# Layer two's odd linear part computed once per token pair: 512 columns become 257, the mirrored half moves to VectorE and GpSimd

## The chip, the cores and the metric

The kernel runs on one core of a Trainium2 chip. A core has TensorE (matmuls, PE in the profile), VectorE (DVE), ScalarE (ACT), GpSimd (POOL) and SyncE (SP, which here only issues DMAs). The engines run side by side; each takes its instructions in the order in which the program gives them, and waits on semaphores where it needs another's result. [...] The metric is the device time of one execution in microseconds.

## The reference

```python
X = np.fft.fft(x, axis=1)          # x: 8 sequences, 3072 tokens, 256 features
X = np.fft.fft(X, axis=2)
a = X.real.reshape(24576, 256)
h = np.maximum(np.maximum(a @ w1, a @ w2), a @ w3)   # 256 -> 768
out = h @ w_out                                      # 768 -> 256
```

So it is a two-dimensional Fourier transform of each sequence, of which the real part goes through a feed-forward layer with a maximum of three projections. The kernel uses two identities. First, max(a w1, a w2, a w3) = a w1 + max(0, a (w2-w1), a (w3-w1)), so that the output is a linear part, a (w1 w_out), plus a hidden part through the 768 features. Second, token s and its mirror token 3072-s of a sequence share their parts: with an even part E and an odd part O, one is made of E + O and the other of E - O. Every matrix is folded with the feature transform beforehand, so the kernel never forms the full transform.

## The kernel before, in words

**Data.** For each of the 8 sequences the class Mix produces a tile t with the even parts tE and the odd parts tO of 1536 token pairs, 128 feature rows each. Row 0 of tO is an exception: it holds the transform's feature 128, which is even, so its sign does not turn for the mirrored token. The constant sgn (line 357) is +1 for row 0 and -1 for the others.

**Blocks, units, slots.** The main loop (line 707) goes over the sequences, and within one over 3 blocks of 512 token pairs. A block has 6 units, one for each group of 128 hidden features; I number them 0 to 5 (and 0 to 17 over a sequence, where the text says "units 13, 15, 17"). A unit is layer one for that group: unit_plus (lines 476, 477) makes the sums of the direct tokens in two PSUM banks with four matmuls; unit_out (490, 491) takes ReLU on ScalarE (tile stmp) and a maximum on VectorE, into hp. unit_minus (484) then adds a difference to the same two banks, of the unit before, which turns them into the sums of the mirrored tokens; unit_out makes hm of these. There are two pairs of banks for this, which the units use in turn.

**Layer two.** A block's layer two, l2_block, runs during the next block's units. It is a Python generator that hands TensorE one matmul for each step; each unit takes ten steps (l2_some(10), line 737), after its own layer one. It goes over the block's 4 slots of 128 token pairs, 0 to 3. For a pair of slots the even linear part is computed into a bank pl (516) and copied to SBUF by ScalarE (even, 520). Per slot a bank po takes: the odd linear part of the direct and of the mirrored tokens in a single matmul of 512 columns (524), the left 256 with the odd weights, the right 256 with the same weights times sgn; then six hidden matmuls of 256 columns from hp into the left half, and six from hm into the right half (500). VectorE adds the even part to both halves (ot, 529). po has two banks, used in turn by the slots (pool ps_o, 644). Two outputs leave: the right half by an indirect DMA that GpSimd issues (534), the left by a DMA on SyncE's queue (544). The last block has a routine of its own, l2_last, so that l2_block handles 23 blocks and 92 slots.

**What else stands in the queues.** After its layer-two steps a unit runs what the plan (line 666 on) puts there: the mix pieces of the next sequence (TensorE, with an eviction on ScalarE; 13 units of 18 have one, units 5 to 17 in most sequences), loads of later sequences on SyncE's queue, and turn_chunk, which casts a quarter of the next but one sequence's rows from fp32 to bf16 on GpSimd, in two instructions (144, 146). For sequences 2 and later these casts are planned in units 13, 15, 17 and unit 1 of the next sequence, or, while sequences 0 and 1 are worked on, in units 14, 16 and units 0 and 2 of the next; sequence 1's own casts are in units 0, 2, 5 and 8 of sequence 0. The order on every engine is the order of these calls: the kernel schedules by hand (line 57).

```python
                l2_some(10)                              # 737, in every unit
            nc.tensor.matmul(po, to[:, cp], gw[:, 256:768], start=True, stop=True)   # 524
```

Of the kernel before, what the change touches and what calls it, by code (L numbers as in the profile page):

```python
# [9 lines left out]
FP32 = mybir.dt.float32  # L10
# [3 lines left out]
ALU = mybir.AluOpType  # L14
# [19 lines left out]
def kernel(  # L34
# [46 lines left out]
    gE = [consts.tile([128, DFF], BF16, name=f"gE{i}", tag=f"gE{i}") for i in range(2)]  # L81
    gO = [consts.tile([128, DFF], BF16, name=f"gO{i}", tag=f"gO{i}") for i in range(2)]
    gD = [consts.tile([128, DFF], BF16, name=f"gD{i}", tag=f"gD{i}") for i in range(2)]
    gw = consts.tile([128, 768], BF16, tag="gw")
    rows_m = consts.tile([128, 12 * B], INT32, tag="rows_m")
    mark = consts.tile([1, 1], FP32, tag="mark")
    sgn = consts.tile([128, 1], FP32, tag="sgn")
    dif = consts.tile([128, 1], FP32, tag="dif")
    t_mid = consts.tile([128, 2, B], BF16, tag="t_mid")
    z_all = consts.tile([128, 128 * 26], BF16, tag="z_all")  # L90
    z = z_all.rearrange("p (c r) -> p c r", r=26)
# [119 lines left out]
    for (name, value) in (("half_pi", 0.5 * math.pi), ("rnd", ROUND), ("n24", -24.0)):  # L211
        c = gen.tile([128, 1], FP32, name=name, tag=name)
        nc.vector.memset(c, value)
        consts_of[name] = c
    nc.vector.memset(z[:, :, 24:26], 0.0)
    nc.vector.memset(m0f[:, 50:52], 0.0)
    nc.vector.memset(m0r[:, 50:52], 0.0)
    half = gen.tile([128, 256], FP32, tag="half")
# [169 lines left out]
    def prep_second():  # L388

        for jp in range(NJC // 2):  # L390
            pst = ps_f.tile([128, 512], FP32, name="pst", tag="ps")
            for k in range(2):
                jc = jp * 2 + k
                for fc in range(2):
                    nc.tensor.matmul(
                        pst[:, k * 256:(k + 1) * 256],
                        w1_bf[:, fc * DFF + jc * 128: fc * DFF + jc * 128 + 128],
                        md[fc], start=(fc == 0), stop=(fc == 1))
            nc.vector.tensor_copy(out=g1t[:, jp * 512:(jp + 1) * 512], in_=pst)
            yield  # L400
        psw = ps_f.tile([128, 512], FP32, name="psw", tag="ps")
        for half in range(2):
            for jc in range(NJC):
                nc.tensor.matmul(
                    psw[:, half * 256:(half + 1) * 256],
                    g1t[:, jc * 256 + half * 128: jc * 256 + half * 128 + 128],
                    wout_bf[:, jc * 256:(jc + 1) * 256],
                    start=(jc == 0), stop=(jc == NJC - 1))
        nc.vector.tensor_copy(out=gw[:, 0:512], in_=psw)
        nc.scalar.activation(out=gw[:, 512:768], in_=psw[:, 256:512], func=AX.Copy, scale=sgn)  # L410
        yield

    class Mix:
# [84 lines left out]
    def l2_hidden(po, hcols):  # L498
        for jc in range(NJC):
            nc.tensor.matmul(po, hcols(jc), wout_bf[:, jc * 256:(jc + 1) * 256],  # L500
                             start=False, stop=(jc == NJC - 1), skip_group_check=True)
            yield

    def l2_block(b, blk, hp, hm, te, to):

        base = b * S
        for sub in range(4):
            slot = blk * 4 + sub
            r = slot + 1
            cp = slice(slot * 128, slot * 128 + 128)  # L510
            sp = slice(sub * 128, sub * 128 + 128)
            if sub % 2 == 0:
                pl = ps_f.tile([128, 512], FP32, name="pl", tag="ps")
                for i in range(2):
                    ci = (slot + i) * 128
                    nc.tensor.matmul(pl[:, i * 256:(i + 1) * 256], te[:, ci:ci + 128],  # L516
                                     gw[:, 0:256], start=True, stop=True)
                    yield
                even = even_pool.tile([128, 512], FP32, name="even", tag="even")
                nc.scalar.copy(out=even, in_=pl)  # L520
            lin = even[:, (sub % 2) * 256:(sub % 2 + 1) * 256]
            po = ps_o.tile([128, 512], FP32, name="po", tag="po")
            ot = out_pool.tile([128, 512], FP32, name="ot", tag="ot")
            nc.tensor.matmul(po, to[:, cp], gw[:, 256:768], start=True, stop=True)  # L524
            yield
            yield
            yield from l2_hidden(po[:, 0:256], lambda jc: hp[:, jc, sp])
            yield from l2_hidden(po[:, 256:512], lambda jc: hm[:, jc, sp])
            nc.vector.tensor_tensor(  # L529
                out=ot.rearrange("p (h c) -> p h c", h=2),  # L530
                in0=po.rearrange("p (h c) -> p h c", h=2),
                in1=lin.unsqueeze(1).to_broadcast([128, 2, 256]), op=ALU.add)
            lo = 1 if r == 12 else 0
            stored(nc.gpsimd.indirect_dma_start(  # L534
                out, bass.IndirectOffsetOnAxis(
                    ap=rows_m[0:128 - lo, b * 12 + slot: b * 12 + slot + 1], axis=0),
                ot[lo:128, 256:512], None), "scattered", ("scattered", "direct"))
            nc.gpsimd.memset(mark, 0.0)
            if r <= 11:
                stores = [(0, 128, base + r)]  # L540
            else:
                stores = [(0, 64, base), (64, 128, base + 12)]
            for (p0, p1, row) in stores:
                stored(nc.sync.dma_start(out=out[row: row + 24 * (p1 - p0 - 1) + 1: 24, :],
                                         in_=ot[p0:p1, 0:256]), "direct", ("scattered",))

    def l2_last(hp, hm, te, to, flipped):

        base = (B - 1) * S
        ter, tor = flipped  # L550
        for sub in (3, 0, 1, 2):
            slot = 8 + sub
            r = slot + 1
            cp = slice(slot * 128, slot * 128 + 128)
            sp = slice(sub * 128, sub * 128 + 128)
            sm = slice((3 - sub) * 128, (4 - sub) * 128)
            po = ps_o.tile([128, 512], FP32, name="po", tag="po")
            ot = out_pool.tile([128, 512], FP32, name="ot", tag="ot")
            for (h, tev, tov, wo, hid) in (
                    (0, te[:, cp], to[:, cp], gw[:, 256:512], lambda jc: hp[:, jc, sp]),  # L560
                    (1, ter[:, sm], tor[:, sm], gw[:, 512:768], lambda jc: hm[:, jc, sm])):
                if sub == 2 and h == 1:
                    po = ps_f.tile([128, 512], FP32, name="pol", tag="ps")
                ph = po[:, h * 256:(h + 1) * 256]
                nc.tensor.matmul(ph, tev, gw[:, 0:256], start=True, stop=False)
                yield
                nc.tensor.matmul(ph, tov, wo, start=False, stop=True)
                yield
                yield from l2_hidden(ph, hid)
                if sub == 2:  # L570
                    nc.vector.tensor_copy(out=ot[:, h * 256:(h + 1) * 256], in_=ph)
            if sub != 2:
                nc.vector.tensor_copy(out=ot, in_=po)
# [70 lines left out]
    ps_o = ctx.enter_context(tc.tile_pool(name="ps_o", bufs=2, space=bass.MemoryType.PSUM))  # L644
    h_pool = ctx.enter_context(tc.tile_pool(name="hbuf", bufs=2))
    out_pool = ctx.enter_context(tc.tile_pool(name="outbuf", bufs=6))
    even_pool = ctx.enter_context(tc.tile_pool(name="evenbuf", bufs=2))
    second = [prep_first(1, lambda: ps_o.tile([128, 512], FP32, name="psg", tag="po")),
              prep_second()]
# [36 lines left out]

    for (u, fn) in ((0, prep_some), (0, prep_some), (1, prep_some), (1, prep_some),
                    (2, lambda: m.k(2)), (2, prep_some), (3, lambda: m.k(3)),
                    (3, prep_some), (4, prep_some), (5, prep_some),
                    (6, lambda: m.k(4)), (7, lambda: m.k(5)), (7, m.end),  # L690
                    (0, lambda: turn_chunk(1, 0)), (2, lambda: turn_chunk(1, 1)),
                    (5, lambda: turn_chunk(1, 2)), (8, lambda: turn_chunk(1, 3))):
        at(0, u, fn)
# [13 lines left out]
    for b in range(B):  # L707
# [15 lines left out]
        for blk in range(3):  # L723
# [7 lines left out]
            for jc in range(NJC):  # L731
# [2 lines left out]
                if prev is not None:  # L734
                    finish(prev)
                prev = (pses, tO[:, cs], jc, hm)
                l2_some(10)
                if b == B - 1 and blk == 0:
                    if jc == 0:
                        middle = l2_mid()  # L740
# [40 lines left out]
```

## Time and profile before

| | us |
|---|---|
| median of 3 runs | 426.62 (426.32 to 426.94) |
| the profiled execution | 426.25 |
| its span, first to last instruction | 424.4 |
| TensorE busy | 404.4 |
| VectorE busy | 275.4 |
| ScalarE busy | 258.9 |
| GpSimd busy | 248.8 |

The span is what the profile covers; what lies around it, 1.8 us here, is not in any row. Busy times are sums of instructions, and a matmul's recorded time overlaps with the next one's, so that the cost of a matmul is read from the starts of neighbours. A group's line gives line number, engine, operation, output and inputs, count, busy time, mean nanoseconds of one, and the idle time ahead of it with the releaser. The clock granted to TensorE was 1.00 in all slices.

### The profile page before, as it was taken

The numbers are of one execution on the slowest core, as the hardware profiler recorded it, in microseconds if no ns is written. First come the engines' busy times: TensorE is split into PE (matmuls) and PEld (weight loads), VectorE is DVE, ScalarE is ACT, GpSimd is POOL, SyncE is SP. The second block draws the span as 40 slices with busy tenths as digits, with TensorE's granted clock in tenths as the row PEclk, the third lists the DMA queues.
The fourth block names the chain that finished last, engine by engine and source line by source line (L and its number), as shares of the span: only waits on it lengthen the run. The fifth ranks groups of instructions, "written<-read, shape, count | busy, mean of one in ns | idle before, by whom it ended". The sixth has DMA issues, their size and how long they took to land.

```text
span 424.4 us, 8690 instructions
## 1 busy us (share of the span) xinstructions
PE 404.4 (95%) x3032; PEld 270.3 (64%) x3087; DVE 275.4 (65%) x456; ACT 258.9 (61%) x478; POOL 248.8 (59%) x295
## 2 busy tenths in 40 slices
PE   0899999999999999999999999999999999999996
PEld 0365666666666666666676666666666666666665
DVE  8857665566656665675666665675656666666773
ACT  5856666566665666656666667657665666654650
POOL 9958746972379625982299525983289622214420
PEclk9999999999999999999999999999999999999999
DMA  9999895694318841496217851388311221111213
GB/s 108 105 172 182 175 222 134 150 225 89 107 64 186 185 126 49 124 218 146 98 62 176 207 132 56 99 200 180 105 53 73 64 69 71 75 51 52 100 71 129
DMA packets 131172, 51.89 MB, mean 122 GB/s; under 512 B 113073, under 2 KB 128184, under 8 KB 131128
## 3 DMA queue, kind: packets, MB, share of 16 engines
q1 hardware_dynamic: 105408, 35.93, 35.8%
q0 software_dynamic: 24784, 15.08, 16.6%
q8 instruction: 24, 0.39, 0.4%
q10 hardware_dynamic: 936, 0.33, 0.3%
q14 instruction: 20, 0.16, 0.1%
HBM read 29.02 MB, written 25.17 MB: 128 GB/s over the span
## 4 chain that ended last, share of the span: by engine, by line
PE 83%; POOL 4%; DVE 3%; issue 3%; DMA 2%; SPq 2%; ACT 2%; DVEq 0%; ACTq 0%; POOLq 0%
PE po L500 28%; PE pse L476 14%; PE pse L484 13%; PE pse L477 12%; PE po L524 4%; POOL x L100 3%; PE pl L516 2%; PE ps L458 2%; PE ps L456 2%; SPq L100 2%; PE ps L432 2%; PE ps L430 2%; ACT stmp L490 1%; DVE ot L529 1%; DMA w_bf<-in_moe_w_dram 1%
## 5 line engine op out<-in xcount | busy, mean ns | idle before, releaser
L490 ACT ACTIVATE stmp<-pse 128x512 bf16<-128x512 f32 x288 | 171.6, 600 | 52.7 <-PE pse L477 39.4
L534 POOL DMA_INDIRECT out_dram<-ot,rows_m x92 | 100.3, 1090 | 159.0 <-DVE ot L529 149.7
L491 DVE TENSOR_TENSOR hp<-pse,stmp 128x512 bf16<-128x512 f32 x144 | 99.5, 691 | 129.2 <-ACT stmp L490 90.8
L476 PE MATMUL pse<-t,gE 128*128 128x512 bf16 x285 | 108.1, 379 | 2.1 <-ACT t L460 0.2
L491 DVE TENSOR_TENSOR hm<-pse,stmp 128x512 bf16<-128x512 f32 x144 | 99.2, 689 | 7.5 <-ACT stmp L490 6.7
L477 PE MATMUL pse<-t,gO 128*128 128x512 bf16 x255 | 96.6, 379 | 0.2
L500 PE MATMUL po<-wout_bf,hp 128*128 128x256 bf16 x576 | 86.1, 273 | 0.3
L484 PE MATMUL pse<-t,gD 128*128 128x512 bf16 x274 | 82.8, 379 | 1.3 <-POOL gD L384 0.9
L500 PE MATMUL po<-wout_bf,hm 128*128 128x256 bf16 x570 | 77.8, 273 | 0.3
L500 PEld LDWEIGHTS <-hp 128*128 128x128 bf16 x576 | 56.3, 98 | 26.2
L500 PEld LDWEIGHTS <-hm 128*128 128x128 bf16 x576 | 56.3, 98 | 16.4
L529 DVE TENSOR_TENSOR ot<-po,even 128x512 f32<-128x512 f32 x92 | 62.8, 683 | 0.0
L146 POOL CAST x<-xs 96x1056 bf16<-96x1056 f32 (+1 forms) x35 | 58.1, 1674 | 0.0
L144 POOL CAST x<-xs 96x1056 bf16<-96x1056 f32 x28 | 56.8, 2028 | 2.3 <-DMA xs<-in_x_dram 2.3
L460 ACT CAST t<-ps 128x512 bf16<-128x512 f32 x47 | 27.5, 585 | 43.3 <-PE ps L458 43.1
L437 ACT CAST z_all<-ps 128x480 bf16<-128x480 f32 x45 | 25.1, 558 | 43.0 <-PE ps L432 43.0
L484 PEld LDWEIGHTS <-gD 128*128 128x128 bf16 x288 | 27.9, 98 | 33.4 <-POOL gD L384 1.4
L477 PEld LDWEIGHTS <-gO 128*128 128x128 bf16 x288 | 28.1, 98 | 19.9 <-issue 1.1
L476 PEld LDWEIGHTS <-gE 128*128 128x128 bf16 x288 | 28.1, 97 | 19.2 <-issue 0.4
L524 PE MATMUL po<-gw,t 128*128 128x512 bf16 x87 | 33.0, 379 | 0.0
L520 ACT COPY even<-pl 128x512 f32<-128x512 f32 x46 | 26.8, 582 | 0.1
L430 PE MATMUL ps<-m24f,x 96*128 96x96 bf16 x224 | 24.7, 206 | 0.0
(147 smaller groups left out, 333.0 us busy)
## 6 DMA issues: line engine op xcount, KB each, us to landing
xs<-in_x_dram SPq DMA_DIRECT2D x84, 198.0 KB
out_dram<-ot SPq DMA_DIRECT2D x90, 128.0 KB
xs<-in_x_dram SPq DMA_DIRECT2D x28, 192.0 KB
out_dram<-ot,rows_m POOLq DMA_INDIRECT x92, 3.0
x<-in_x_dram POOLq DMA_DIRECT2D x12, 96.0 KB, 4.1
w_bf<-in_moe_w_dram POOLq DMA_DIRECT2D x6, 192.0 KB, 4.8
out_dram<-ot SPq DMA_DIRECT2D x17, 64.0 KB
xs<-in_x_dram SPq DMA_DIRECT2D x32, 5.8 KB
```

The source lines that it names most:

```text
L144: nc.gpsimd.tensor_copy(v[:, 0:33, ch * 32:ch * 32 + 32], xs[:, 0:32 * 64].rearrange("p (bb dl) -> p dl bb", dl=64)[:, 0:33, :])
L146: reverse(lambda out, in_: nc.gpsimd.tensor_copy(out, in_), v[:, 33:66, :], xs, ch * 32, 33 if ch == 3 else 32)
L430: nc.tensor.matmul(ps1[:, c0:c0 + n], x0[0](d), mf[:, 0:n], start=True, stop=False)
L476: nc.tensor.matmul(pse[:, 0:n], gE[i][:, js], te, start=True, stop=False)
L477: nc.tensor.matmul(pse[:, 0:n], gO[i][:, js], to, start=False, stop=True)
L484: nc.tensor.matmul(pse, gD[i][:, js], to, start=False, stop=True, skip_group_check=True)
L490: nc.scalar.activation(out=stmp[:, 0:n], in_=pses[0][:, 0:n], func=AX.Relu)
L491: nc.vector.tensor_tensor(out=dst, in0=src3, in1=stmp[:, 0:n], op=ALU.max)
L500: nc.tensor.matmul(po, hcols(jc), wout_bf[:, jc * 256:(jc + 1) * 256], start=False, stop=(jc == NJC - 1), skip_group_check=True)
L524: nc.tensor.matmul(po, to[:, cp], gw[:, 256:768], start=True, stop=True)
L529: nc.vector.tensor_tensor(out=ot.rearrange("p (h c) -> p h c", h=2), in0=po.rearrange("p (h c) -> p h c", h=2), in1=lin.unsqueeze(1).to_br ...
L534: stored(nc.gpsimd.indirect_dma_start(out, bass.IndirectOffsetOnAxis(ap=rows_m[0:128 - lo, b * 12 + slot: b * 12 + slot + 1], axis=0), ot[ ...
```

## The change

The matmul of 512 columns for the odd linear part is replaced by one of 257: the odd weights (256 columns) and one column that picks row 0 of tO, feature 128 of each token, as column 256 of the bank. The mirrored half follows from the direct one: sum of sgn times t times W is twice the row 0 term less the direct sum. VectorE computes that from the bank, with a constant tile twice (two times row 0 of the odd weights, on all partitions) and column 256 as a scalar for each partition, into an SBUF tile named other. GpSimd adds other to the even part, into the second half of a wider even tile, and VectorE's ot addition then takes 512 plain columns. Since the bank's columns 256 to 511 are no longer written by the odd matmul, the six hm matmuls start them; column 256 already holds the feature, and twice is less by one there.

The odd matmul of the next slot is issued between the six hp and the six hm steps of the slot before (function l2_odd), so that VectorE's pass can run ahead. With 56 steps in a block the units take 10, 9, 9, 10, 9, 9 of them. One more preparation step makes twice at the start, from two small constants that VectorE sets.

```diff
+    nc.vector.memset(two_row, 0.0)
+    nc.vector.memset(two_row[0:1], 2.0)
+    nc.vector.memset(gw[:, 512:513], 0.0)
+    nc.vector.memset(gw[0:1, 512:513], 1.0)
...
+        pst = ps_f.tile([128, 512], FP32, name="pst", tag="ps")
+        nc.tensor.matmul(pst[:, 0:256], two_row, gw[:, 256:512], start=True, stop=True)
+        nc.vector.tensor_copy(out=twice, in_=pst[:, 0:256])
+        nc.vector.tensor_scalar(out=twice[:, 0:1], in0=twice[:, 0:1], scalar1=-1.0, scalar2=None,
+                                op0=ALU.add)
...
+    def l2_odd(b, slot):
+
+        po = ps_o.tile([128, 512], FP32, name="po", tag="po")
+        nc.tensor.matmul(po[:, 0:257], mixes[b].tO[:, slot * 128:slot * 128 + 128], gw[:, 256:513],
+                         start=True, stop=True)
+        other = other_pool.tile([128, 256], FP32, name="other", tag="other")
+        nc.vector.scalar_tensor_tensor(out=other, in0=twice, scalar=po[:, 256:257],
+                                       in1=po[:, 0:256], op0=ALU.mult, op1=ALU.subtract)
+        odd[b, slot] = po, other
...
+            if (b, slot) not in odd:
+                l2_odd(b, slot)
+                yield
...
-                even = even_pool.tile([128, 512], FP32, name="even", tag="even")
-                nc.scalar.copy(out=even, in_=pl)
-            lin = even[:, (sub % 2) * 256:(sub % 2 + 1) * 256]
-            po = ps_o.tile([128, 512], FP32, name="po", tag="po")
+                even = even_pool.tile([128, 1024], FP32, name="even", tag="even")
+                nc.scalar.copy(out=even.rearrange("p (i c) -> p i c", i=2)[:, :, 0:256],
+                               in_=pl.rearrange("p (i c) -> p i c", i=2))
+            lin = even[:, (sub % 2) * 512:(sub % 2 + 1) * 512]
+            po, other = odd.pop((b, slot))
+            nc.gpsimd.tensor_tensor(out=lin[:, 256:512], in0=lin[:, 0:256], in1=other, op=ALU.add)
             ot = out_pool.tile([128, 512], FP32, name="ot", tag="ot")
-            nc.tensor.matmul(po, to[:, cp], gw[:, 256:768], start=True, stop=True)
-            yield
-            yield
             yield from l2_hidden(po[:, 0:256], lambda jc: hp[:, jc, sp])
+            after = (b, slot + 1) if slot < 11 else (b + 1, 0)
+            if after < (B - 1, 8):
+                l2_odd(*after)
+                yield
             yield from l2_hidden(po[:, 256:512], lambda jc: hm[:, jc, sp])
-            nc.vector.tensor_tensor(
-                out=ot.rearrange("p (h c) -> p h c", h=2),
-                in0=po.rearrange("p (h c) -> p h c", h=2),
-                in1=lin.unsqueeze(1).to_broadcast([128, 2, 256]), op=ALU.add)
+            nc.vector.tensor_tensor(out=ot, in0=po, in1=lin, op=ALU.add)
...
+    other_pool = ctx.enter_context(tc.tile_pool(name="otherbuf", bufs=2))
...
-                l2_some(10)
+                l2_some(9 + (jc % 3 == 0))
```

More of the change, by code (lines that the diff above doesn't have):

```diff
@@ L83 @@
     gD = [consts.tile([128, DFF], BF16, name=f"gD{i}", tag=f"gD{i}") for i in range(2)]
-    gw = consts.tile([128, 768], BF16, tag="gw")
+    gw = consts.tile([128, 770], BF16, tag="gw")
     rows_m = consts.tile([128, 12 * B], INT32, tag="rows_m")
     mark = consts.tile([1, 1], FP32, tag="mark")
+    two_row = consts.tile([128, 128], BF16, tag="two_row")
     sgn = consts.tile([128, 1], FP32, tag="sgn")
     dif = consts.tile([128, 1], FP32, tag="dif")
+    twice = consts.tile([128, 256], FP32, tag="twice")
     t_mid = consts.tile([128, 2, B], BF16, tag="t_mid")
@@ L409, in prep_second @@
         nc.vector.tensor_copy(out=gw[:, 0:512], in_=psw)
-        nc.scalar.activation(out=gw[:, 512:768], in_=psw[:, 256:512], func=AX.Copy, scale=sgn)
+        nc.scalar.activation(out=gw[:, 514:770], in_=psw[:, 256:512], func=AX.Copy, scale=sgn)
+        yield
[4 more added lines that the diff above has]
+                                op0=ALU.add)
         yield
@@ L502, in l2_hidden @@
             yield
+    odd = {}
+    def l2_odd(b, slot):
[6 more added lines that the diff above has]
+        odd[b, slot] = po, other
     def l2_block(b, blk, hp, hm, te, to):
@@ L509, in l2_block @@
             r = slot + 1
-            cp = slice(slot * 128, slot * 128 + 128)
             sp = slice(sub * 128, sub * 128 + 128)
+            if (b, slot) not in odd:
+                l2_odd(b, slot)
+                yield
             if sub % 2 == 0:
@@ L518, in l2_block @@
                     yield
-                even = even_pool.tile([128, 512], FP32, name="even", tag="even")
-                nc.scalar.copy(out=even, in_=pl)
-            lin = even[:, (sub % 2) * 256:(sub % 2 + 1) * 256]
-            po = ps_o.tile([128, 512], FP32, name="po", tag="po")
+                even = even_pool.tile([128, 1024], FP32, name="even", tag="even")
[4 more added lines that the diff above has]
+            nc.gpsimd.tensor_tensor(out=lin[:, 256:512], in0=lin[:, 0:256], in1=other, op=ALU.add)
             ot = out_pool.tile([128, 512], FP32, name="ot", tag="ot")
-            nc.tensor.matmul(po, to[:, cp], gw[:, 256:768], start=True, stop=True)
-            yield
-            yield
             yield from l2_hidden(po[:, 0:256], lambda jc: hp[:, jc, sp])
+            after = (b, slot + 1) if slot < 11 else (b + 1, 0)
+            if after < (B - 1, 8):
+                l2_odd(*after)
+                yield
             yield from l2_hidden(po[:, 256:512], lambda jc: hm[:, jc, sp])
-            nc.vector.tensor_tensor(
-                out=ot.rearrange("p (h c) -> p h c", h=2),
-                in0=po.rearrange("p (h c) -> p h c", h=2),
-                in1=lin.unsqueeze(1).to_broadcast([128, 2, 256]), op=ALU.add)
+            nc.vector.tensor_tensor(out=ot, in0=po, in1=lin, op=ALU.add)
             lo = 1 if r == 12 else 0
@@ L560, in l2_last @@
                     (0, te[:, cp], to[:, cp], gw[:, 256:512], lambda jc: hp[:, jc, sp]),
-                    (1, ter[:, sm], tor[:, sm], gw[:, 512:768], lambda jc: hm[:, jc, sm])):
+                    (1, ter[:, sm], tor[:, sm], gw[:, 514:770], lambda jc: hm[:, jc, sm])):
                 if sub == 2 and h == 1:
@@ L688 @@
                     (2, lambda: m.k(2)), (2, prep_some), (3, lambda: m.k(3)),
-                    (3, prep_some), (4, prep_some), (5, prep_some),
+                    (3, prep_some), (4, prep_some), (5, prep_some), (5, prep_some),
                     (6, lambda: m.k(4)), (7, lambda: m.k(5)), (7, m.end),
```

## The prediction

> **What bounds the kernel now.** I read the page first: engine totals, then the chain.
>
> ```profile
> PE 404.4 (95%) x3032; PEld 270.3 (64%) x3087; DVE 275.4 (65%) x456; ACT 258.9 (61%) x478; POOL 248.8 (59%) x295
> ...
> PE 83%; POOL 4%; DVE 3%; issue 3%; DMA 2%; SPq 2%; ACT 2%; DVEq 0%; ACTq 0%; POOLq 0%
> ```
>
> TensorE carries the chain. The other engines have a third of the span free, but an average says nothing about when. So I took the groups of instructions by line, for the prices of what is touched:
>
> ```profile
> L491 DVE TENSOR_TENSOR hm<-pse,stmp 128x512 bf16<-128x512 f32 x144 | 99.2, 689 | 7.5 <-ACT stmp L490 6.7
> ...
> L524 PE MATMUL po<-gw,t 128*128 128x512 bf16 x87 | 33.0, 379 | 0.0
> ```
>
> A matmul's 379 ns overlaps the next one; what it costs is the pitch, which only the timeline shows. This is unit 3 of a block, in the middle of the span (start, length, engine, line), TensorE first, then VectorE:
>
> ```profile
> 246.22 0.81 PE L476 MATMUL pse<-t,gE 128*128 128x512 bf16 x2
> ...
> 247.52 0.38 PE L516 MATMUL pl<-gw,t 128*128 128x256 bf16 x2
> 247.74 0.38 PE L524 MATMUL po<-gw,t 128*128 128x512 bf16 x1
> 247.96 0.82 PE L500 MATMUL po<-wout_bf,hp 128*128 128x256 bf16 x6
> ```
>
> ```profile
> 247.52 0.69 DVE L491 TENSOR_TENSOR hp<-pse,stmp 128x512 bf16<-128x512 f32 x1 [1.50 <-ACT stmp L490]
> 248.14 0.69 DVE L491 TENSOR_TENSOR hm<-pse,stmp 128x512 bf16<-128x512 f32 x1
> 248.74 0.68 DVE L529 TENSOR_TENSOR ot<-po,even 128x512 f32<-128x512 f32 x1
> ```
>
> Pitches: 512 columns 0.22 us (more exactly 0.215, four L476/L477 in 0.86), 256 columns 0.109 (two L516 in 0.22). TensorE issues without a gap. Counted from a unit's first matmul T, the six matmuls of layer one end at T+1.29, and VectorE starts hp at T+1.29, hm at T+1.91 and the addition ot at T+2.52, ending T+3.20. VectorE takes its work in program order.
>
> Last, GpSimd's timeline, where the next sequence's rows are cast:
>
> ```profile
> 260.73 0.96 POOL L534 DMA_INDIRECT out_dram<-ot,rows_m  x1 [4.27 <-DVE ot L529]
> 261.70 0.09 POOL L538 MEMSET mark<- 1x1 f32 x1
> 261.73 2.06 POOL L144 CAST x<-xs 96x1056 bf16<-96x1056 f32 x1
> 263.73 2.08 POOL L146 CAST x<-xs 96x1056 bf16<-96x1056 f32 x1
> ...
> 267.39 2.04 POOL L144 CAST x<-xs 96x1056 bf16<-96x1056 f32 x1
> 269.38 2.06 POOL L146 CAST x<-xs 96x1056 bf16<-96x1056 f32 x1
> 271.60 0.98 POOL L534 DMA_INDIRECT out_dram<-ot,rows_m  x1 [0.16 <-issue]
> ```
>
> Between 261.7 and 283 us GpSimd is nearly full. Today nobody waits for it there: it only stores.
>
> **The change part by part.**
>
> (1) TensorE. 92 matmuls of 512 columns become 257 columns: 92 x (0.215 - 0.109) = -9.8 us. A 257th column I price as 1/256 more; the bounds are 0.109 and 0.215, and it is nearest to the first. Steps per block go from 60 to 56, so a unit lasts 2.27 to 2.38 us without a mix piece and 2.70 to 2.81 with one (0.435).
>
> (2) A new wait for the accumulator bank. po has two banks, so slot n+1 needs the bank of slot n-1, free after ot(n-1). Before, slot n+1's matmul came after all of slot n; now it comes between slot n's hp and hm steps. With 15, 13, 15 and 13 steps for the four slots and 10, 9, 9, 10, 9, 9 per unit, slot 1's last hm matmul is the last step of unit 2, so ot(1) is issued in unit 3, behind that unit's hp and hm: it ends at T+3.20. TensorE reaches slot 3's odd matmul in the same unit, after two pl and six hp steps: T+1.29+8x0.109 = T+2.16. The release takes 0.14 more (the first warm-up matmul starts at 12.51, the VectorE write it waits for ends at 12.37). Stall 3.20+0.14-2.16 = 1.17 us. Queued behind it on TensorE are the rest of the unit, the mix piece and the next unit. The other three slots are free of it: ot(0) is in unit 1 and its bank is wanted in unit 2 at T+1.51, 0.5 us after the read; the other two have more. Each of the 23 blocks that l2_block handles has one unit 3: 23 x 1.17 = +26.9 us. Bounds: 0.9 (no release delay, VectorE's 0.61 pitch for ot instead of 0.68, rounding) to 1.3 per block.
>
> (3) VectorE gains 92 passes of 128x256 from PSUM. Rows: 128x384 casts take 552 ns, 128x512 691, so by that line 0.41; the SCALAR_TENSOR_TENSOR rows (768: 1.01, 896: 1.15) give 0.45. Taken: 0.43. Hidden: hp, hm, pass and ot at their pitches need 2.3 us, only units 3 and 5 have both pass and ot, and they last 2.38 plus the stall of (2) and, but for the last sequence, 2.70. If that cover goes, hm comes late and layer one's third matmul (T+0.43 of the next unit) waits; today it has 0.17 us to spare in the short units. The wider even tile and the plain ot addition keep their element counts: nothing.
>
> (4) GpSimd gains 92 additions of 128x256, and here VectorE, which never waited for GpSimd in layer two, starts to: ot(n) needs add(n), which stands in GpSimd's queue behind the indirect store of slot n-1, behind whatever cast was issued between. Price of an add: no two-operand row exists. Casts give 1.76 ns an element over 0.18 (1056 in 2.03, 32 in 0.23), so 0.63; the TENSOR_SCALAR rows (384 in 1.24, 8 in 0.34) give 2.4 over 0.32, so 0.93. I take the middle, 0.77. [...]
>
> Outside the cast stretches it fits: ot(n-1) ends, +0.27 (252.24 to 252.51 in the trace) store 0.98, add 0.77, 0.1 release: 2.2 us, and from one ot's end to the next one's start it is 2.4 to 4.5 us with mix pieces (2.0 at the least without, in the last sequence: 0.2 lost there). Within them each link is cast pair 4.08 + 0.16 + store 0.98 + mark and add 0.83 = 6.1 us for one slot, where a slot has 3.9. Laid out for sequences 2 to 5 (casts in units 13, 15, 17 and 1; zero is the start of unit 13; unprimed slots are of the second block, primed of the third):
>
> add(1) ends 5.3, cast to 9.4, add(2) 11.35, cast to 15.45, add(3) 17.4, cast to 21.5, add(0') 23.5, add(1') 26.35, cast to 30.6, add(2') 32.6.
> With the stall of (2), VectorE would come to ot(1) at 7.9, ot(2) 11.9, ot(3) 15.05: that one waits until 17.5. TensorE, at slot 1's odd matmul at 16.97, waits for its bank until 18.34: 1.37. Then ot(0') would start 21.2, starts 23.6; slot 2's matmul waits 22.44 to 24.41: 1.97. ot(1') is in time; ot(2') starts 32.7 instead of 31.2, and the next block's first matmul waits 1.03. With 0.1 at a layer-one matmul: 4.5 us a stretch, four stretches, 18.0.
> For the first two sequences the casts come in units 14, 16, 0 and 2: the same bookkeeping gives 0.70, 2.01 (on top of that unit's 1.17) and 2.26, 5.0 a stretch, 9.9 for both. The lone cast beside the first block costs about 0.8. Sum +28.7 us; with the add at 0.63 about 23, at 0.93 about 35.
>
> (5) Start: four more small VectorE memsets before the tables (rows of 0.06 to 0.17, pitches 0.03 to 0.14) and one short matmul: +0.4 at most, taken.
>
> Sum: 424.4 - 9.8 + 26.9 + 28.7 + 0.4 = 470.6 span. The profiled execution took 426.25 for its 424.4, so 1.8 lies around the span: 472.4. The median of before, 426.62, is 0.4 above the profiled one: 472.8.
>
> **The rivals.**
>
> A, both waits are hidden and only the columns count: 426.6 - 9.8 + 0.4 = 417.2. The place is slot 3's bank in unit 3. For it speaks that L524 shows no idle time now with the same two banks. It decides where all new waiting is under 9.4 us, 0.41 a block: ot(1) would have to end by T+2.4, before VectorE has finished hm. Against it: ot(1) stands behind hp and hm in one queue.
>
> B, only the bank wait, GpSimd's additions arriving in time: 426.6 - 9.8 + 26.9 + 0.4 = 444.1. It needs a link of 6.1 us to fit 3.9 plus the reserve of ot, about 1.3; the casts' rows speak against.
>
> C, only GpSimd's lateness: 426.6 - 9.8 + 28.7 + 0.4 = 445.9. It needs ot(1) off the path, as in A.
>
> D, worse. An add of 1.2 us lengthens every link by 0.43: five and a half such per stretch, 2.4 x 6 = 14, and outside the casts ot(3) would wait some 0.2 to 0.5 in most blocks: 490 to 495. A second way there is the clock: the granted clock is 1.00 in every slice now, and the longest wait listed for TensorE after its start is 1.4 us, while my longest new gap is 3.2 us, and some eight are of 2 us or more. If half speed followed each for some 3 us, that is 1.5 us each, 12 us: 485. [...]
>
> **How the numbers follow.** My case 0.67, own range 460 to 484 (the add's bounds and 0.9 to 1.3 for the bank). A 0.09, B 0.10, C 0.05, D 0.08, and 0.01 for an end within 0.2% of before (about what a measurement of this kernel tells from no change). The range 443 to 484 takes in B and C and leaves out A, D and the tails. Faster 0.09, same 0.01, slower 0.90.
>
> **What would show it.** The odd matmul's line at 0.11 us pitch: (1). One TensorE gap near 1.2 us per block at slot 3's odd matmul, released by ot: (2). Idle time of VectorE before ot put down to GpSimd's addition, beside casts only: (4). GpSimd's additions at 0.6 to 0.9. The prediction is wrong if TensorE has no idle time before the odd matmul, if GpSimd orders its casts otherwise, or if the additions are far from 0.77.

## The result, and the profile after

The changed kernel takes 469.18 us (median of four runs, 468.74 to 469.68) against 426.50 for the kernel before on the same chip (426.32 to 426.94): a ratio of 1.0996, 95% interval 1.098 to 1.1013. The profiled execution took 468.95 us, and its span is 467.1 us, 42.7 us more than before.

The page of the changed kernel: engine totals, then the chain by engine.

```profile
PE 405.3 (87%) x3033; PEld 271.2 (58%) x3088; DVE 312.9 (67%) x554; ACT 259.4 (56%) x478; POOL 314.4 (67%) x387
...
PE 46%; POOL 21%; issue 12%; DVE 8%; DMA 6%; ACT 4%; SPq 2%; POOLq 0%; DVEq 0%; ACTq 0%
```

TensorE's share of the chain fell from 83% to 46%, GpSimd's rose from 4% to 21%. (TensorE's busy sum did not fall, although the work did: the last matmul ahead of each wait counts with its whole recorded time (0.27 us at a pitch of 0.11), where before the next one overlapped it, and 6.8 us at the start, 23.9 to 30.7, ran at a granted clock of 0.50.) The groups by line, busy and mean ns, then the idle time ahead and its releaser; first the row of ot in the kernel before, then three rows of the changed kernel:

```profile
L529 DVE TENSOR_TENSOR ot<-po,even 128x512 f32<-128x512 f32 x92 | 62.8, 683 | 0.0
```

```profile
L558 DVE TENSOR_TENSOR ot<-po,even 128x512 f32<-128x512 f32 x92 | 63.0, 685 | 35.0 <-POOL even L550 34.4
...
L550 POOL TENSOR_TENSOR even<-even,other 128x256 f32<-128x256 f32 x92 | 67.2, 730 | 0.5 <-ACT even L546 0.5
...
L521 PE MATMUL po<-gw,t 128*128 128x257 bf16 x92 | 25.3, 275 | 37.9 <-DVE ot L558 37.9
```

TensorE now stands idle ahead of the odd matmul (L521) for 37.9 us in 37 waits, all released by ot; and ot itself waits 34.4 us for GpSimd's addition (L550). Idle time in these rows begins where the last matmul's modelled end lies, some 0.17 us behind the time at which the next one could have started. Measured from start to start, less the pitch of the matmul before, the 37 gaps are 44.0 us (37.9 + 37 x 0.165).

Unit 3 of a block away from the casts (its first matmul is at 166.72), TensorE and then VectorE, from the timeline:

```profile
166.72 0.81 PE L488 MATMUL pse<-t,gE 128*128 128x512 bf16 x2
...
168.01 0.38 PE L542 MATMUL pl<-gw,t 128*128 128x256 bf16 x2
168.23 0.82 PE L512 MATMUL po<-wout_bf,hp 128*128 128x256 bf16 x6
169.97 0.28 PE L521 MATMUL po<-gw,t 128*128 128x257 bf16 x1 [0.92 <-DVE ot L558]
```

```profile
168.01 0.69 DVE L503 TENSOR_TENSOR hp<-pse,stmp 128x512 bf16<-128x512 f32 x1 [1.00 <-ACT stmp L502]
168.63 0.69 DVE L503 TENSOR_TENSOR hm<-pse,stmp 128x512 bf16<-128x512 f32 x1
169.24 0.68 DVE L558 TENSOR_TENSOR ot<-po,even 128x512 f32<-128x512 f32 x1
```

VectorE goes through hp, hm and ot without a pause. TensorE could have issued the odd matmul at 168.88 (six hp steps of 0.109 from 168.23) and issued it at 169.97: 1.09 us. Such a wait stands once in every one of the 23 blocks; in the first it is 0.97, and in two it is merged with the wait for a late addition. ot ends at 169.92 by its row, so that the release takes about 0.06 us.

And a stretch with casts (the first of the four that are planned with sequences 2 to 5; its unit 13 begins at 178.63), GpSimd first, then the ot and the odd matmul that follow:

```profile
195.02 0.73 POOL L550 TENSOR_TENSOR even<-even,other 128x256 f32<-128x256 f32 x1
195.69 1.98 POOL L146 CAST x<-xs 96x1056 bf16<-96x1056 f32 x1
197.63 2.01 POOL L148 CAST x<-xs 96x1056 bf16<-96x1056 f32 x1
199.79 1.01 POOL L560 DMA_INDIRECT out_dram<-ot,rows_m  x1 [0.16 <-issue]
200.80 0.09 POOL L564 MEMSET mark<- 1x1 f32 x1
200.86 0.73 POOL L550 TENSOR_TENSOR even<-even,other 128x256 f32<-128x256 f32 x1
```

```profile
201.62 0.69 DVE L558 TENSOR_TENSOR ot<-po,even 128x512 f32<-128x512 f32 x1 [2.28 <-POOL even L550]
...
202.37 0.27 PE L521 MATMUL po<-gw,t 128*128 128x257 bf16 x1 [1.67 <-DVE ot L558]
```

One link of the chain: two casts, the store, the mark, the addition. ot waits 2.28 us for it and TensorE, behind ot, 1.83 by the starts.

The accounting, all from starts of matmuls in the two traces:

| term | predicted | measured |
|---|---|---|
| columns of the odd matmul | -9.8 | -9.8 (by the pitches) |
| bank wait at slot 3, 23 blocks | +26.9 | +25.0 (22 x 1.09 and 0.97) |
| additions late beside casts | +28.7 | +18.9 |
| making twice, and the first pass | +0.4, start in all | +2.4 |
| the rest of the start | in the same 0.4 | +6.0 |
| a gap ahead of the first matmul on gD, there before (at 38.72), gone | - | -1.0 |
| sum | +46.2 | +41.5 (span: +42.7) |

The 18.9 are what the 44.0 us of gaps leave after the bank wait: about 3.3 us in each of the four stretches of sequences 2 to 5 (0.75, 1.83, 0.75), and 2.0 and 3.6 in those of the first two sequences. The 2.4 are two gaps in the first blocks: 0.95 ahead of the matmul that makes twice (it waits for the weights gw) and 1.48 ahead of the first hp matmul, where VectorE's first pass is late. A rest of 1.2 us I cannot place. The 6.0 us were in no term of the prediction: TensorE's first layer-one matmul starts at 33.36 us and started at 27.32 before.

### The profile page after: what moved, and what is told of

It is laid out like the page before. It is cut to its first block, busy times and chain, and to the rows that moved or that the text cites. A ratio compares the mean times of both kernels' runs of the same rounds, so it can differ in the third digit from the quotient of the medians.

```text
span 467.1 us, 8957 instructions
## 1 busy us (share of the span) xinstructions
PE 405.3 (87%) x3033; PEld 271.2 (58%) x3088; DVE 312.9 (67%) x554; ACT 259.4 (56%) x478; POOL 314.4 (67%) x387
## 4 chain that ended last, share of the span: by engine, by line
PE 46%; POOL 21%; issue 12%; DVE 8%; DMA 6%; ACT 4%; SPq 2%; POOLq 0%; DVEq 0%; ACTq 0%
PE po L512 14%; PE pse L488 8%; PE pse L496 6%; PE pse L489 6%; POOL x L148 6%; POOL out_dram L560 6%; POOL even L550 5%; DVE ot L558 4%; POOL x L146 4%; ACT stmp L502 3%; DMA x<-in_x_dram 3%; DMA xs<-in_x_dram 2%; PE ps L442 2%; PE po L521 2%; PE ps L444 2%
## 5 line engine op out<-in xcount | busy, mean ns | idle before, releaser
L560 POOL DMA_INDIRECT out_dram<-ot,rows_m x92 | 102.4, 1113 | 127.4 <-DVE ot L558 119.5
L558 DVE TENSOR_TENSOR ot<-po,even 128x512 f32<-128x512 f32 x92 | 63.0, 685 | 35.0 <-POOL even L550 34.4
L512 PE MATMUL po<-wout_bf,hm 128*128 128x256 bf16 x570 | 85.4, 273 | 0.1
L512 PEld LDWEIGHTS <-hm 128*128 128x128 bf16 x576 | 56.3, 98 | 33.5 <-issue 17.1
L550 POOL TENSOR_TENSOR even<-even,other 128x256 f32<-128x256 f32 x92 | 67.2, 730 | 0.5 <-ACT even L546 0.5
L521 PE MATMUL po<-gw,t 128*128 128x257 bf16 x92 | 25.3, 275 | 37.9 <-DVE ot L558 37.9
L449 ACT CAST z_all<-ps 128x480 bf16<-128x480 f32 x45 | 25.2, 559 | 54.8 <-PE ps L444 54.8
L524 DVE SCALAR_TENSOR_TENSOR other<-twice,po 128x256 f32<-128x256 f32 x92 | 44.1, 479 | 9.8 <-PE po L521 9.7
```

The source lines that it names most:

```text
L524: nc.vector.scalar_tensor_tensor(out=other, in0=twice, scalar=po[:, 256:257], in1=po[:, 0:256], op0=ALU.mult, op1=ALU.subtract)
L550: nc.gpsimd.tensor_tensor(out=lin[:, 256:512], in0=lin[:, 0:256], in1=other, op=ALU.add)
L558: nc.vector.tensor_tensor(out=ot, in0=po, in1=lin, op=ALU.add)
L560: stored(nc.gpsimd.indirect_dma_start(out, bass.IndirectOffsetOnAxis(ap=rows_m[0:128 - lo, b * 12 + slot: b * 12 + slot + 1], axis=0), ot[ ...
```

## The experiments

**Without the additions.** The first experiment takes the two large terms apart. In this kernel VectorE's ot adds the even part to both halves, as before the change, and GpSimd's addition is gone; it leaves out the odd linear part of the mirrored tokens.

```diff
-            nc.gpsimd.tensor_tensor(out=lin[:, 256:512], in0=lin[:, 0:256], in1=other, op=ALU.add)
...
-            nc.vector.tensor_tensor(out=ot, in0=po, in1=lin, op=ALU.add)
+            nc.vector.tensor_tensor(
+                out=ot.rearrange("p (h c) -> p h c", h=2),
+                in0=po.rearrange("p (h c) -> p h c", h=2),
+                in1=lin[:, 0:256].unsqueeze(1).to_broadcast([128, 2, 256]), op=ALU.add)
```

> The changed kernel without GpSimd's addition: ot adds the even part alone to both halves, as before the change, so the mirrored tokens lack their odd linear part; everything else, VectorE's pass over the bank included, stays. Theory 'casts delay the additions': the gaps beside the casts go (18.9 us in all), the 23 of 1.09 us stay: 450 us. Rival 'the pass and the earlier matmul alone make all waits': 469; rival 'GpSimd's part is everything': 426 or less.

Measured: 450.18 us against 428.12 for the kernel before on that chip, a ratio of 1.0524 (1.0482 to 1.0565). Its list of waits (engine, line, what it waits for; us in total, times, longest):

```profile
PEld L521 <- DVE ot L557: 26.5, 22, 1.2
...
PE po L521 <- DVE ot L557: 21.2, 23, 0.9
```

These are exactly 23 waits of nearly one length: by the starts the first is 0.97 and the other 22 are 1.09, 25.0 together, and no other gap is left at the odd matmul. So the bank wait is one thing and the late additions another, and the additions account for the whole rest of the gaps.

**The steps in another order.** The bank wait should come from where slot 3's odd matmul falls. Here unit 2 has ten steps and unit 3 nine. Slot 1 is done after 28 steps, and its ot is issued when the 29th is taken: that now falls into unit 2, ahead of hp and hm of unit 3.

```diff
-                l2_some(9 + (jc % 3 == 0))
+                l2_some((10, 9, 10, 9, 9, 9)[jc])
```

> The changed kernel with 10, 9, 10, 9, 9, 9 steps for the units instead of 10, 9, 9, 10, 9, 9: unit 2 takes one step more, and with it ot of slot 1 is issued there, a unit ahead of slot 3's odd matmul. Theory 'bank wait behind hp and hm in VectorE's queue': the 23 gaps of 1.09 us at slot 3's odd matmul go. Outside the cast stretches that is 11 to 12 of them, 12 us; inside, GpSimd's chain sets the pace and takes most of the other 13 back: 455 to 458 us. If the two causes simply added up: 444. Rival (the wait has another releaser than ot's place in the queue, the pass over the bank for example): the gaps stay, 469.

Measured: 460.89 against 428.12, a ratio of 1.0757 (1.0724 to 1.079). The changed kernel would be at 470.8 on that chip (1.0996 x 428.1), so the order is worth 9.9 us here, not the 25 that the regular gaps hold, and less than the 13 to 16 that were expected. Its list of waits:

```profile
DVE ot L558 <- POOL even L550: 54.8, 41, 3.6
...
PE po L521 <- DVE ot L558: 28.3, 20, 2.7
```

The regular gaps are gone away from the casts (20 gaps instead of 37, 31.5 us by the starts instead of 44.0, and a single one of 1.09, in the first block). But beside the casts the gaps of a stretch, which were 0.75, 1.83 and 0.75, are now 1.9, 1.85 and 1.5, and ot waits 54.8 us for GpSimd instead of 34.4. While TensorE waited at slot 3 of each block, GpSimd's chain caught up; with the wait gone, TensorE comes to the same late addition sooner. The two terms are not independent: they add in the changed kernel because the bank wait comes first. Some 3 us more went to two stretches at half clock (3.41 us each, so about 1.7 us lost in each; the granted clock is 0.57 over 97 to 101 us and 0.72 over 150 to 156); they are taken up at the end. Without them the time would lie in the expected 455 to 458.

**The start.** The change adds tiles and two columns to gw. Every tile that is allocated behind gw moves up by 1312 bytes in each partition, which is no multiple of 256 (1312 = 5 x 256 + 32). To see whether that alone costs anything, this kernel is the one before, with only those tiles added and nothing that uses them:

```diff
-    gw = consts.tile([128, 768], BF16, tag="gw")
+    gw = consts.tile([128, 770], BF16, tag="gw")
...
+    two_row = consts.tile([128, 128], BF16, tag="two_row")
...
+    twice = consts.tile([128, 256], FP32, tag="twice")
```

> The kernel before, with nothing but the three SBUF tiles of the change sized or added (gw 770 columns, two_row, twice, the last two unused), so that every tile behind them lies 1312 bytes further, 32 past a multiple of 64 instead of on one. No instruction is added. Theory 'addresses': the first unit, which came 6.0 us later in the changed kernel, comes 5 to 6 us later here too, because the DMA writes of the first rows take longer (128-byte packets 68 ns instead of 32 on average), so 431 to 433 us. Rival 'instructions' (the four added memsets, or chance in that run): 426.5, first unit at 27.3.

And the other way round, the changed kernel with gw at 896 columns, which puts the tiles back to the same place in a 512-byte line:

```diff
-    gw = consts.tile([128, 770], BF16, tag="gw")
+    gw = consts.tile([128, 896], BF16, tag="gw")
```

> The changed kernel with gw widened to 896 columns, of which 770 are used, so that the tiles behind lie at the same places modulo 512 bytes as before the change. Theory 'addresses': the first unit starts at 27.5 to 28 instead of 33.4, the rest is as it was: 462.5 to 464 us. Rival 'instructions' or chance: 469.

Measured: the kernel before with moved tiles takes 432.86 against 428.12, a ratio of 1.0102 (1.0071 to 1.0133): 4.7 us for two tiles and two columns that nothing reads. The changed kernel with the places restored takes 464.57, a ratio of 1.0843 (1.0807 to 1.0879), 1.4% less than the change as it was made (1.0843 to 1.0996). The queue rows of the pages (packets, MB, the time of the packets as a share of 16 engines' span), first the kernel before, then the changed kernel, then the kernel before with moved tiles, then the changed kernel with restored places:

```profile
q1 hardware_dynamic: 105408, 35.93, 35.8%
q0 software_dynamic: 24784, 15.08, 16.6%
```

```profile
q1 hardware_dynamic: 105408, 35.93, 44.4%
q0 software_dynamic: 24784, 15.08, 22.2%
```

```profile
q1 hardware_dynamic: 105408, 35.93, 47.2%
q0 software_dynamic: 24784, 15.08, 24.4%
```

```profile
q1 hardware_dynamic: 105408, 35.93, 33.4%
q0 software_dynamic: 24784, 15.08, 15.1%
```

The packets and bytes are the same, and with the places restored they take a quarter to a third less time than in the changed kernel. The first mix matmul, in the same order:

```profile
21.11 0.21 PE L430 MATMUL ps<-m24f,nat 96*128 96x96 bf16 x1
```

```profile
23.97 0.24 PE L442 MATMUL ps<-m24f,nat 96*128 96x96 bf16 x1 [2.35 <-DVE nat L325]
```

```profile
23.98 0.20 PE L432 MATMUL ps<-m24f,nat 96*128 96x96 bf16 x1 [2.16 <-DVE nat L321]
```

```profile
21.89 0.21 PE L442 MATMUL ps<-m24f,nat 96*128 96x96 bf16 x1
```

VectorE's tile nat is made of rows that a DMA brings; they land later (VectorE waits 3.48 us for them in the changed kernel and starts the copy of 1056 columns into back at 17.16 us, before at 12.96), and TensorE has nothing to do meanwhile. With the places restored the first layer-one matmul starts at 28.10 instead of 33.36, so that 5.3 of the 6.0 us are the tiles' places. Of these, 2.1 are the later first mix matmul (23.97 to 21.89); the other 3.2 fall in the 6.8 us at half clock (0.50, 23.9 to 30.7) that follow the wait of 2.35 us in the changed kernel and do not occur with the places restored.

Which distance counts? Three more kernels are the one before with gw widened to 800, 832 and 896 columns, which moves all that stands behind it by 64, 128 and 256 bytes:

> The kernel before with gw widened from 768 to 800 columns, nothing else: the tiles behind lie 64 bytes further. If what slows the DMA writes is a place off a multiple of 64 bytes, packets of 128 and 256 bytes take 32 and 18 ns as before and the time is that of before. If it is a place off a multiple of 256 or 512, packets take longer and the time is 2 to 6 us above.

> The kernel before with gw 832 columns wide: the tiles behind lie 128 bytes further, nothing else. The 128-byte writes of the first rows still fill whole 128-byte cells then. If cells of 128 bytes count, they take 32 ns as before and the first unit starts at 27 to 28; if cells of 256 or 512 bytes count for the whole row, the packets of 256 bytes (18 ns before) and the time move as with 64 bytes, 2 to 5 us above before.

> The kernel before with gw 896 columns wide: 256 bytes further. Two of the four xs buffers lie at such places already in the kernel before, so no packet should be slower: the time of before. If it is slower, 512 is what counts, and the kernel before pays already for two of its four buffers.

| moved by | ratio to before (95%) | 128-byte packet, mean ns | 256-byte packet, mean ns |
|---|---|---|---|
| 0 (the kernel before) | 1 | 32.0 | 19.9 |
| 1312 = 5 x 256 + 32 | 1.0102 (1.0071 to 1.0133) | 69.7 | 28.8 |
| 64 | 1.0088 (1.0055 to 1.0121) | 66.1 | 25.6 |
| 128 | 1.0054 (1.0023 to 1.0085) | 33.1 | 23.6 |
| 256 | 0.999 (0.9963 to 1.0017) | 32.0 | 20.0 |

The packet times are means over the packet records of these traces (128 bytes: queue q0; 256 bytes: q1). Of these moves only the one by 256 bytes costs nothing (0.999). At 128 the packets of 128 bytes are as fast as ever (33.1 ns against 32.0) and those of 256 are not (23.6 against 19.9): these times fit a boundary every 256 bytes, counted from the places in the kernel before, and a packet is slow where it lies across one. The single packets say the same. Rows of 128 bytes lie 128 bytes apart, so that a move by 64 takes only every second one across such a boundary; in that trace 57% of the 10752 packets took 30 to 34 ns as ever, and the others more, many of them over 100 ns. In the changed kernel, moved by 1312, it is 57% too, and 18% took over 100 ns; in the kernel before, 99.8% took 30 to 34.

**Three things undone.** With the places restored, the other step order and no additions, only the true cost of the change should be left, and the gain of the columns:

> The changed kernel with the places modulo 512 restored (gw 896 wide), unit 2 taking the extra step, and without GpSimd's addition (so the mirrored tokens lack their odd linear part). If bank wait, late additions and places are all there is besides the columns, what stays is -9.8 us for the columns, +2.9 for the preparation of twice (gaps of 0.95 and 1.48 us before the first block, 0.4 more at the start): 6 to 7 us under the kernel before of the same chip. Rival 'something else costs, VectorE's pass for one': at the time of before or above it.

Measured: 421.15 against 427.12, a ratio of 0.9857 (0.9828 to 0.9887). That is -6.0 us: the columns' -9.8, and 3.9 of gaps in its first blocks that the kernel before does not have (0.95 and 1.48 for twice and the first pass, 1.09 at the first block's slot 3, and 0.4 more than before ahead of the first matmul on gD). Nothing later in the kernel takes more than some tenths of a us from it.

**The additions moved ahead of the casts.** Last, the complete computation without the waits. For slots 1 and 3 the addition is issued with the odd matmul, half a slot sooner; the casts lie three units apart instead of two and begin earlier.

```diff
-            nc.gpsimd.tensor_tensor(out=lin[:, 256:512], in0=lin[:, 0:256], in1=other, op=ALU.add)
+            if sub % 2 == 0:
+                nc.gpsimd.tensor_tensor(out=lin[:, 256:512], in0=lin[:, 0:256], in1=other, op=ALU.add)
...
                 l2_odd(*after)
+                if sub % 2 == 0:
+                    nc.gpsimd.tensor_tensor(out=even[:, 768:1024], in0=even[:, 512:768],
+                                            in1=odd[after][1], op=ALU.add)
...
-            folds = begin[b] + 8 if b else 14
+            folds = 6 if b else 12
...
-                at(b, folds + (0, 2, 4, 6)[ch], lambda b=b, ch=ch: turn_chunk(b + 2, ch))
+                at(b, folds + (0, 3, 6, 9)[ch], lambda b=b, ch=ch: turn_chunk(b + 2, ch))
```

One kernel has this with the restored places (steps 10, 9, 9, 10, 9, 9 as in the change), the other has the other step order too, and two preparation steps one unit earlier.

> As the version with the additions ahead and the casts spread, places restored, but with the units' steps as in the change (10, 9, 9, 10, 9, 9) and its preparation. Theory: the 23 gaps of 1.09 us at slot 3's odd matmul are there, none beside the casts: 17 to 19 us above before of the same chip. Rival 'both kinds of gap have one cause': the 1.09 gaps go too, at or under before.

> A complete version: places restored, unit 2 with the extra step, the addition for a block's slots 1 and 3 issued with their odd matmul, so ahead of the indirect store of the slot before, the casts in units 6, 9, 12, 15 (sequences 0 and 1: 12, 15, 18, 21 of sequence 0) instead of 13, 15, 17, 19, and the sum psw formed one unit earlier than twice needs it. GpSimd's queue is then addition, addition, cast pair, store, store for two slots: 8.0 us for three units of 8.1. Theory: no addition stands behind a store and a cast together, no gap at the odd matmuls is left, 8 to 9.5 us under the kernel before of the same chip. Rival 'GpSimd is simply too busy beside casts': gaps of 0.5 to 2 us stay beside the casts, and the time is at or above before.

Measured: the first 445.40 against 427.12 (+18.3), a ratio of 1.0418 (1.0385 to 1.0451), with the 23 gaps (22 of 1.09, the first 0.97) and none beside the casts. The second 420.94 against 427.12, a ratio of 0.9853 (0.9828 to 0.9878): it is 1.5% faster than the kernel before. Between the two lie 24.5 us, nearly all from one line of step counts (the two preparation steps are the only other difference); the same line gave 9.9 where the casts took the rest back. GpSimd's timeline in the second:

```profile
209.28 0.73 POOL L551 TENSOR_TENSOR even<-even,other 128x256 f32<-128x256 f32 x1
209.96 0.72 POOL L558 TENSOR_TENSOR even<-even,other 128x256 f32<-128x256 f32 x1
210.63 2.02 POOL L146 CAST x<-xs 96x1056 bf16<-96x1056 f32 x1
212.61 2.02 POOL L148 CAST x<-xs 96x1056 bf16<-96x1056 f32 x1
214.79 1.01 POOL L564 DMA_INDIRECT out_dram<-ot,rows_m  x1 [0.16 <-issue]
```

Two slots' additions stand ahead of the casts, and only the store behind them, for which nobody waits. Its engine totals and its group of ot:

```profile
PE 395.1 (94%) x3033; PEld 270.4 (65%) x3088; DVE 310.7 (74%) x554; ACT 259.2 (62%) x478; POOL 313.5 (75%) x387
...
L562 DVE TENSOR_TENSOR ot<-po,even 128x512 f32<-128x512 f32 x92 | 62.7, 682 | 0.1
```

GpSimd and VectorE are as busy as in the changed kernel to within 1%, in a span 48 us shorter: what cost most of the time was the order of their work, not its amount. I had expected 8 to 9.5 us of gain and 6.2 came; what is missing stands in the first blocks (by the starts 1.42 at the first hp matmul, 1.09 at the first block's slot 3, 1.0 and 0.4 ahead of two layer-one matmuls at 43 and 44 us).

## Why the prediction came out as it did

The likeliest case is the one that happened: both waits are exposed, the clock stays up nearly everywhere (0.993 on the mean), and the kernel takes 469.2 us instead of 472.8. But the small error is the sum of larger ones of both signs, and in that it is luck: 11.7 us too much in the two waits, 8 too little at the start.

(1) The columns: right. Where nothing stops the next matmul, it starts 0.11 behind the odd one (49.83 to 49.94).

(2) The bank wait: right in its mechanism, its place, its count and nearly its size. ot(1) runs third in VectorE's queue of unit 3 and TensorE stands at slot 3's odd matmul. The term that was off is the release: I had put 0.14 behind ot's end, taken from the start-up, and it is 0.06. So the wait is 1.09 and not 1.17, which makes 1.9 us over 23 blocks.

(3) VectorE's pass: its rows have 0.48 where 0.43 was taken. It is hidden as forecast, but for its first occurrence (1.48, below).

(4) The additions: the mechanism is right. ot waits for GpSimd beside the casts and nowhere else, and without the additions no such gap is left. The term of 28.7 was mis-sized by 9.8, and for this reason. An addition's row shows 0.73, but the next instruction of GpSimd starts 0.67 behind it, where I had priced 0.77 by the middle of the casts' and the scalar rows; with the shorter release a link is some 0.15 shorter. In the stretch laid out, the ends of the additions came at 5.3, 11.2, 17.1 and 23.0 against 5.3, 11.35, 17.4 and 23.5. TensorE in turn came 0.1 to 0.4 later to its waits than reckoned. A gap is the small difference of two long chains, so that 0.3 to 0.5 us in their ends took 4.5 to 3.3 in each stretch. In the first two sequences, where 5.0 each were put down, it was 2.0 and 3.6: there the first gap of 0.70 does not occur, and the two that do are 0.3 to 1.5 shorter. The 0.8 put down for the lone cast beside the first block did not come either.

(5) The start: wrong. "+0.4 at most" counted the added instructions. It missed what waits for them (the matmul for twice waits 0.95 for the weights, the first hp matmul 1.48 for VectorE's first pass), and it put nothing down for the 6.0 us by which the first unit comes later, 5.3 of them from the tiles' places, since the diff shows two more columns in gw and no instruction that could be slower.

The rivals. A needed ot(1) off the path and the additions in time; the second version of the last experiment has both, by other orders, and there the change is worth 6 us where it costs 43 as made. B is what the kernel without additions shows: 1.0524, which is 449 us on the 426.6 of before, where B said 444.1 and had 0.4 for the start. C needed the bank wait gone and the lateness as it is; the nearest kernel is the one with the other step order, and it shows that C's term grows when B's goes. My case had them as a plain sum, which is true only in the order that the change has. D's addition of 1.2 us did not come (0.67). D's half speed of some 3 us behind each long gap was the author's estimate, and no trace of the kernel before shows such a stretch. In the changed kernel the granted clock stayed at 1.00 behind the longest new gap, of 2.70, and fell to 0.50 for 6.8 us at the start; the last section has what the other runs show.

## What to carry to other kernels

Work moved to an engine with time to spare is not free when the work stands in a queue behind long items that nobody used to wait for: lay out that queue for the stretch where it is full, and move the short instruction ahead of the long ones. Where two buffers alternate, find out in which unit a buffer is read and in which it is wanted again; one step moved from unit 3 to unit 2 was worth 24.5 us here once the additions came in time, and 9.9 us while they did not. And a change that adds a tile moves all tiles behind it: compare the DMA rows of the two profiles even where no DMA was touched, and keep the sizes of tiles in front of DMA targets at multiples of 256 bytes (a move by 256 cost nothing here, 0.999, and those by 64, 128 and 1312 cost 0.5 to 1.0%).

## What the runs showed that was not expected

**The place of a tile set the speed of the DMA that wrote it.** The table above: in the traces in which rows of 128 bytes lie across 256-byte boundaries, packets of that size took 66 to 70 ns on the mean instead of 32; where rows of 256 bytes do, their packets took 24 to 29 instead of 20. It mattered above all at the start, where TensorE waits for the first rows: in the profiled execution with moved tiles, 4.5 of the 7.7 us that its units fall behind are there with the first unit, the rest comes in three later waits, and from 152 us on nothing is added.

**Half clock after gaps of 2.5 to 2.9 us.** In the changed kernel with restored places TensorE has a gap of 2.72 us by the starts (2.56 in the row), and some 1.1 us after its end the granted clock falls to 0.50 for 3.4 us. The timeline, and then the stretch behind (us, busy and count for PE, PEld, DVE, ACT, POOL, then the granted clock):

```profile
146.52 0.28 PE L521 MATMUL po<-gw,t 128*128 128x257 bf16 x1 [2.56 <-DVE ot L558]
```

```profile
148.00:151.00 3.00, 3.00 (x12) 1.82 (x12) 1.39 (x2) 0.60 (x1) 2.83 (x4) 0.50 0.99 176
```

In the changed kernel itself a gap of 2.70 at nearly the same place has no such sequel:

```profile
151.30 0.28 PE L521 MATMUL po<-gw,t 128*128 128x257 bf16 x1 [2.54 <-DVE ot L558]
```

```profile
150.00:156.00 6.00, 4.13 (x24) 2.46 (x26) 2.52 (x4) 2.39 (x4) 5.83 (x7) 1.00 1.01 135
```

The kernel with the other step order has it twice, after gaps of 2.53 and 2.89. In all twelve traces, the changes of the granted clock lie whole multiples of 3.41 us apart (in the changed kernel at 23.92, 30.74 and 467.65 us: 2 and 128 times 3.41). Laid against a grid of that step, the two gaps differ. This is the 3.41 us stretch of the kernel with restored places ahead of its half clock (144.23 to 147.65), and then the two stretches of the changed kernel between which its gap falls:

```profile
144.23:147.65 3.42, 1.13 (x6) 0.64 (x8) 1.18 (x3) 0.27 (x1) 3.42 (x5) 1.00 1.00 179
```

```profile
146.80:150.21 3.41, 1.96 (x14) 1.08 (x11) 1.69 (x3) 1.67 (x3) 3.24 (x4) 1.00 0.97 165
150.21:153.62 3.41, 2.27 (x15) 1.51 (x17) 2.01 (x4) 1.19 (x2) 3.41 (x3) 1.00 1.05 137
```

In the first, TensorE is idle for 2.29 of the 3.42 us; in the other two, for 1.45 and 1.14, because the grid's edge at 150.21 cuts the gap in two. All twelve traces divide in this way: each of their 21 falls from full to half clock (those behind the last matmul included) stands right behind a stretch with at least 2.16 us idle, and in all other stretches at full clock TensorE was idle for 1.82 us at most. No stretch here has an idle time between the two.
